# Weight conversion spread over the units, set-up coefficients on GpSimd, in a fused attention and two-MoE kernel

## The chip, the cores and the metric

The kernel runs on one core of one Trainium2 chip. The metric is the device time of one execution in microseconds (us); lower is better. Times of the kernel before are the median and the extremes of three runs, and one further execution that was profiled.

## The reference, cut to what is computed

```
state = alpha[:, :, t, :, None] * state + einsum('bhd,bhe->bhde', k[:, :, t], v[:, :, t])
y[:, :, t] = einsum('bhd,bhde->bhe', q[:, :, t], state)
...
h = x @ w_in
P = a[0] + a[1] * h + a[2] * h2 + a[3] * h3
Q = 1.0 + abs(b[0]) * abs(h) + abs(b[1]) * h2
x2 = (P / (Q + 1e-06)) @ w_out
...
e = exp(h - h_max)
solu = h * e / (sum(e) + 1e-09)
out = layernorm(solu) * g_ln @ w_out
```

A linear attention with a decay per channel (batch 4, 8 heads, 768 steps, width 48) feeds a first layer pair of 384 to 2048 to 384 with a rational function between them, and that feeds a second pair of 384 to 1024 to 384. The last `h`, `w_out` and `out` are the second pair's own. All 3072 tokens go through everything. The matrices come as 64-bit floats.

## The kernel before, in words

**Chunks, halves, units.** The 768 steps are cut into six chunks of 128. A chunk is 512 tokens, 128 of each batch entry. The attention works on half chunks of two batch entries: half 0 and half 1 make chunk 0, half 2 and half 3 chunk 1, and so on to half 11; half 4 is the fifth. The first layer pair works on units. A unit is one chunk of 512 tokens against 128 of the 2048 middle columns, so a chunk has 16 units, and there are 96.

**A unit.** `m_up` (lines 642 to 684) does nine matmuls into a PSUM tile `hp` (line 648), nine because weights and tokens are kept as a high and a low part and three products are added over three row blocks. Then comes a chain: ScalarE writes `ah`, `p` and `w` (lines 653 to 656), VectorE and ScalarE alternate (lines 666 to 679), ScalarE writes the high part `gh` (line 681), GpSimd the low part `gl` (line 682). `MIX(u)` picks one of two forms of the chain: for a mixed unit (lines 666 to 672) VectorE has three passes and GpSimd two more, for another (lines 674 to 679) VectorE has four and GpSimd none. `fin[u]` is the last VectorE pass of the chain (line 672 or 679); it is the last to read `hp`. There are three `hp` buffers, so the matmuls of unit u wait for `fin[u-3]`. `m_down` (lines 686 to 703) adds the unit's share to the output, nine matmuls (line 693), and is written four units behind.

**Conversion of the first pair's weights.** A tile of 64-bit words becomes a 32-bit float by three integer passes on VectorE (lines 540, 543, 544; the first two write `fp`, the third `ft`). ScalarE copies the high part (line 555), and GpSimd subtracts it for the low part (line 560). The weights lie in four groups, one for four units of each chunk, with seven tiles in each: three of `w_in` (512 columns) and four of `w_out` (384 columns). Groups 0 and 1 are converted ahead of unit 0 (`w1_group`), groups 2 and 3 during the units of the first chunk (`w1_slots`, line 585): the loop takes two tiles a unit, group 2 in units 0 to 3 and group 3 in units 4 to 7. For group 2 `fp` is a PSUM tile of the pool `at`, for group 3 it is the SBUF tile `ft` itself. The same passes also convert the second pair's weights from unit 15 on, one tile at a time through `st` (`w2_split`).

**Halves.** Halves 0 and 1 are turned on TensorE with scans on VectorE (`a_turn`, line 343). From half 2 on `a_dve` (line 291) prepares a half on VectorE by block transposes and scans, GpSimd makes the last product (line 327), and the result goes to DRAM (`qk_d`, line 329) and back (`qks`, line 268). `a_pe` (line 396) then does the scores `sc` (line 413), the outputs `y` and the state `u`. `half_steps(i)` interleaves the matmuls of half i with the preparation of half i+1; `HOLD` gives the unit from which that preparation may begin: `{2: (4, 2), 3: (13, 2)}` means that half 3 is prepared from unit 4 on, and half 4 from unit 13.

**Order.** The order of each engine's instructions is settled when the program is built, by a scheduler that works on its own estimate of times. `tc.issue_after(x)` keeps what is written inside it behind the instruction x. `later(n)` uses that with `fin[u-n]`. With `G1 = 99` it holds nothing back in the conversion. Loads go out on one queue (SyncE, SPq in the rows) in the order that the scheduler set.

**Set-up.** `consts` (line 111) loads the coefficients `a` and `b` and makes small vectors of them, 24 instructions of one to four columns on VectorE and ScalarE. `PRE` says how many tiles of group 0 are taken at four places between the loads of halves 0 and 1.

```
if fast and u < NF1:
    if f % 4 == 0:
        _run(prep)
        if f:
            stage["bank"] = ""
        prep = w1_slots(f // 4 + 2) if f < 8 else iter(())
    with later(G1):
        take(prep, 1)
m_up(u)
if fast and u < NF1:
    with later(G1):
        take(prep, 1)
```

Of the kernel before, what the change touches and what calls it, by code (L numbers as in the profile page):

```python
# [30 lines left out]
def kernel(  # L31
# [79 lines left out]
    def consts():  # L111


        nc.sync.dma_start(out=ab, in_=bass.AP(moe_a.tensor, moe_a.offset, [[0, 128], [1, 4]]))
# [7 lines left out]
        nc.vector.tensor_scalar(sign, sign, 1.0, None, ALU.subtract)
        nc.vector.tensor_tensor(lin[:, 1:2], ab[:, 2:3], sign, ALU.mult)
        nc.vector.tensor_tensor(base[:, 1:2], ab[:, 1:2], sign, ALU.mult)
        nc.vector.tensor_tensor(a0s, ab[:, 0:1], sign, ALU.mult)
        nc.vector.memset(base[:, 0:1], QC)
        nc.vector.tensor_scalar(bad[:, 4 * NCH:4 * NCH + 2], cf, C_MIN, None, ALU.is_lt)
        nc.vector.tensor_scalar(cf, cf, C_MIN, None, ALU.max)
# [2 lines left out]
        nc.vector.tensor_tensor(t, beta, beta, ALU.mult)
        nc.vector.tensor_tensor(t, t, cf, ALU.mult)
        nc.vector.tensor_scalar(bad[:, 4 * NCH + 2:], t, BETA * BETA, None, ALU.is_gt)
        nc.vector.tensor_scalar(beta, beta, B_MAX, -B_MAX, ALU.min, ALU.max)
        nc.vector.tensor_tensor(t, beta, beta, ALU.mult)
        nc.vector.tensor_tensor(base, base, rc, ALU.mult)
        nc.vector.tensor_tensor(rest, base, t, ALU.subtract)
# [975 lines left out]
```

## Time and profile before

| what | value |
|---|---|
| median of three runs | 781.0 us (779.27 to 783.73) |
| profiled execution, its own time | 778.71 us |
| its span, first to last instruction | 776.7 us |
| TensorE busy | 731.5 us, 94% of the span |
| VectorE busy | 628.9 us, 81% |
| ScalarE busy | 540.3 us, 70% |
| GpSimd busy | 362.5 us, 47% |
| mean granted TensorE clock | 0.97 |

The profile names engines PE (TensorE), DVE (VectorE), ACT (ScalarE), POOL (GpSimd) and SP (SyncE). A timeline row has the start in us, the time of one or of a merged run of instructions in us, engine, line, operation, output<-inputs, shapes, the count, and in brackets the idle time in front of it and what ended that. The shares above are means over very different stretches: about 80 us in which the attention's first halves and half of the first pair's weights are prepared, the 96 units to about 560 us, and the second pair behind them.

### The profile page before, as it was taken

To read this page: it belongs to the slowest core of one execution; us is meant where nothing else is said; L and a number is where in the kernel's file an instruction comes from. 1 tells how busy PE (TensorE), PEld (TensorE's weight loads), DVE (VectorE), ACT (ScalarE), POOL (GpSimd) and SP (SyncE) were. 2 spreads that over 40 slices of the span, in tenths; PEclk is the share of its full clock that TensorE was granted. 3 is DMA by queue.
4 is the path that set the end of the run, shared out by engine and by line. 5 is a ranking of instruction groups with operands and counts; after the bars stand their busy time and mean duration, and the time that the engine had idled before them with its cause. 6 is when DMAs were issued, how large, how long until landed. Compare 5 with 4: busy or idle time off the path is not lost.

```text
span 776.7 us, 13952 instructions
## 1 busy us (share of the span) xinstructions
PE 731.5 (94%) x4988; PEld 608.4 (78%) x4988; DVE 628.9 (81%) x1097; ACT 540.3 (70%) x998; POOL 362.5 (47%) x314
## 2 busy tenths in 40 slices
PE   4865989999999999999999999999999999999996
PEld 4754777878887787778877788888888989988996
DVE  5997999979998989989898876478887698877630
ACT  3446867867977888788878887788965555555541
POOL 4464878666654355434544433342243343452322
PEclk9957999999999999999999999999999999999999
DMA  7999324275737382717544340730025353541653
GB/s 177 289 295 279 61 81 111 89 224 169 186 121 166 114 207 88 184 47 219 124 144 102 124 82 1 281 127 1 1 82 120 101 131 91 129 111 49 140 118 78
DMA packets 87279, 101.75 MB, mean 131 GB/s; under 512 B 34464, under 2 KB 63136, under 8 KB 87200
## 3 DMA queue, kind: packets, MB, share of 16 engines
q1 hardware_dynamic: 87104, 100.67, 48.0%
q8 instruction: 41, 0.67, 0.4%
q14 instruction: 38, 0.31, 0.1%
q10 hardware_dynamic: 96, 0.10, 0.0%
HBM read 60.59 MB, written 27.56 MB: 113 GB/s over the span
## 4 chain that ended last, share of the span: by engine, by line
DVE 18%; PE 18%; ACT 6%; DMA 3%; SPq 3%; issue 2%; POOL 1%; ACTq 0%; DVEq 0%; POOLq 0%
PE x2p L693 6%; PE hp L648 6%; DVE room L807 3%; SPq L817 3%; DVE room L790 2%; ACT jk L792 2%; PE op L831 2%; DVE sm L786 2%; DVE room L805 2%; PE h L767 2%; DMA L<-room 1%; DVE sm L802 1%; DVE sm L803 1%; DVE p L674 1%; DVE sm L804 1%
## 5 line engine op out<-in xcount | busy, mean ns | idle before, releaser
L682 POOL TENSOR_TENSOR gl<-p,gh 128x512 fp32r<-128x512 f32 x96 | 128.4, 1338 | 198.7 <-ACT gh L681 110.6
L648 PE MATMUL hp<-xt,g 128*128 128x512 f32 x432 | 115.3, 410 | 8.4 <-DVE p L672 7.8
L648 PE MATMUL hp<-xt,w 128*128 128x512 f32 x432 | 110.0, 397 | 4.4 <-DVE p L679 4.4
L648 PEld LDWEIGHTS hp<-xt,g 128*128 128x128 f32 x432 | 82.9, 196 | 29.3 <-DVE p L672 8.0
L831 PE MATMUL op<-w2oh,ln 128*128 128x384 f32 x384 | 101.9, 339 | 0.6 <-DVE ln L823 0.6
L693 PE MATMUL x2p<-gh,g 128*128 128x512 f32 x288 | 100.2, 399 | 2.3 <-ACT x2e L701 2.3
L823 POOL TENSOR_TENSOR ln<-L,ln 128x1024 fp32r<-128x1024 f32 x22 | 54.5, 2482 | 100.8 <-ACT ln L822 96.4
L648 PEld LDWEIGHTS hp<-xt,w 128*128 128x128 f32 x432 | 81.1, 190 | 23.6 <-DVE p L679 5.7
L677 DVE SCALAR_TENSOR_TENSOR w<-w,co,hp 128x512 f32<-128x512 f32 x84 | 62.0, 738 | 44.8 <-ACT hp L676 44.1
L693 PE MATMUL x2p<-gh,w 128*128 128x512 f32 x288 | 96.5, 392 | 0.0
L767 PE MATMUL h<-w2ih,x 128*128 128x512 f32 x288 | 90.8, 394 | 0.0
L655 ACT ACTIVATE p<-hp,co 128x512 f32<-128x512 f32 x96 | 65.8, 685 | 11.1 <-POOL gl L682 10.8
L676 ACT ACTIVATE hp<-ah 128x512 f32<-128x512 f32 x84 | 50.1, 596 | 32.9 <-DVE p L674 32.0
L831 PEld LDWEIGHTS op<-w2oh,ln 128*128 128x128 f32 x384 | 70.1, 188 | 2.2 <-DVE ln L823 1.0
L674 DVE SCALAR_TENSOR_TENSOR p<-p,co,hp 128x512 f32<-128x512 f32 x84 | 61.8, 736 | 9.7 <-ACT p L655 9.1
L656 ACT ACTIVATE w<-ah,co 128x512 f32<-128x512 f32 x96 | 69.3, 723 | 0.4
L693 PEld LDWEIGHTS x2p<-gh,g 128*128 128x128 f32 x288 | 54.6, 191 | 17.5 <-ACT x2e L701 5.0
L653 ACT ACTIVATE ah<-hp 128x512 f32<-128x512 f32 x96 | 56.6, 589 | 14.5 <-PE hp L648 11.5
L681 ACT ACTIVATE gh<-p 128x512 fp32r<-128x512 f32 x96 | 59.9, 624 | 7.9 <-DVE p L679 5.1
L831 PE MATMUL op<-w2ol,ln 128*128 128x384 f32 x192 | 65.0, 339 | 0.0
L693 PEld LDWEIGHTS x2p<-gh,w 128*128 128x128 f32 x288 | 54.1, 188 | 11.7
L767 PEld LDWEIGHTS h<-w2ih,x 128*128 128x128 f32 x288 | 53.9, 188 | 11.7
(183 smaller groups left out, 1569.7 us busy)
## 6 DMA issues: line engine op xcount, KB each, us to landing
L<-room SPq DMA_DIRECT2D x96, 128.0 KB, 2.3
qk_d<-qk SPq DMA_DIRECT2D x10, 771.0 KB, 4.1
st<-in_moe_w_out_dram SPq DMA_DIRECT2D x18, 384.0 KB, 5.0
st<-in_moe_w_in_dram SPq DMA_DIRECT2D x12, 512.0 KB, 4.9
qks<-qk_d SPq DMA_DIRECT2D x20, 257.0 KB, 5.0
ra<-in_alpha_dram SPq DMA_DIRECT2D x48, 96.0 KB, 2.3
rk<-in_k_dram SPq DMA_DIRECT2D x48, 96.0 KB, 2.7
rq<-in_q_dram SPq DMA_DIRECT2D x48, 96.0 KB, 2.4
```

The lines of the kernel that those rows point to most:

```text
L648: last["PE", u] = nc.tensor.matmul(hp, lhsT=wi[n](w, kt, o), rhs=xts[c][:, kt, xx, :], start=(kt == 0 and w == 0 and xx == 0), stop=(kt == ...
L653: nc.scalar.activation(ah, hp, AF.Abs)
L655: nc.scalar.activation(p, hp, AF.Square, bias=co[:, 7:8])
L656: nc.scalar.activation(w, ah, AF.Square, bias=co[:, 6:7])
L674: nc.vector.scalar_tensor_tensor(p, p, a1, hp, ALU.add, ALU.mult)
L677: nc.vector.scalar_tensor_tensor(w, w, rest, hp, ALU.add, ALU.mult)
L681: last["ACT", u] = nc.scalar.activation(gh, p, AF.Copy)
L682: last["POOL", u] = nc.gpsimd.tensor_tensor(gl, p, gh[:].bitcast(F32), ALU.subtract)
L693: nc.tensor.matmul(x2ps[c][d], lhsT=wo[n](w, o, d), rhs=gg, start=(f == 0 and w == 0 and gg is gh), stop=(f == NF1 - 1 and w == 1),)
L767: nc.tensor.matmul(hp[:, 512 * n:512 * n + 512], lhsT=x2s[c][:, kt, x, CH * b:CH * b + CH], rhs=w2[w][:, kt, 512 * n:512 * n + 512], start ...
L823: (nc.vector if s in FASTS else nc.gpsimd).tensor_tensor(lo, L, hi.bitcast(F32), ALU.subtract)
L831: nc.tensor.matmul(op, lhsT=x[:, 128 * f:128 * f + 128], rhs=w2[w][:, f, :], start=(f == 0 and x is hi and w == "oh"), stop=(f == NF2 - 1 ...
```

## The change

- Groups 2 and 3 are taken as one sequence, one tile a unit from unit 1 to unit 15 without unit 11 (`PACE`), after the unit's `m_up`, and held behind `fin[u-2]` (from unit 12 on behind `fin[u-1]`). Their loads are written in units 0 and 3 (`w1_fetch`).
- Units 0 and 2 are no longer mixed.
- The coefficients are computed on GpSimd, one reciprocal excepted, and this is written behind the matmuls of half 0. ScalarE's absolute values become products with a sign.
- The second tile of group 0 is no longer loaded ahead of half 1.
- The preparation of half 4 may begin at unit 14.

```
-    HOLD = {2: (4, 2), 3: (13, 2)}
+    HOLD = {2:(4,2),3:(14,2)}
...
-    PRE = (1, 1, 0, 0)
+    PRE = (1, 0, 0, 0)
...
-    G1 = 99
+    G1 = 2
+    PACE = {u: 1 for u in range(1, 16) if u != 11}
     G2 = 3
-    MIX = lambda u: u < 24 and u % 2 == 0
+    MIX = lambda u: 3 < u < 24 and u % 2 == 0
...
-        nc.scalar.activation(babs, bb, AF.Abs)
+
+    def coefficients():
+
+        sb = const.tile([128, 2], F32, name="sb")
+        nc.gpsimd.tensor_scalar(sb, bb, 0.0, 2.0, ALU.is_ge, ALU.mult)
+        nc.gpsimd.tensor_scalar(sb, sb, 1.0, None, ALU.subtract)
+        nc.gpsimd.tensor_tensor(babs, bb, sb, ALU.mult)
...
-        nc.scalar.activation(cf[:, 0:1], bb[:, 1:2], AF.Abs)
-        nc.scalar.activation(cf[:, 1:2], ab[:, 3:4], AF.Abs)
-        nc.scalar.activation(lin[:, 0:1], bb[:, 0:1], AF.Abs)
-        nc.vector.tensor_scalar(sign, ab[:, 3:4], 0.0, 2.0, ALU.is_ge, ALU.mult)
...
+        nc.gpsimd.tensor_copy(cf[:, 0:1], babs[:, 1:2])
+        nc.gpsimd.tensor_copy(lin[:, 0:1], babs[:, 0:1])
+        nc.gpsimd.tensor_scalar(sign, ab[:, 3:4], 0.0, 2.0, ALU.is_ge, ALU.mult)
...
         nc.vector.reciprocal(rc, cf)
-        nc.vector.scalar_tensor_tensor(beta, lin, 0.5, rc, ALU.mult, ALU.mult)
...
+        nc.gpsimd.tensor_scalar(beta, lin, 0.5, None, ALU.mult)
+        nc.gpsimd.tensor_tensor(beta, beta, rc, ALU.mult)
...
-        def w1_slots(n):
+        words2 = {}
+
+        def w1_fetch(n):
...
+            words2[n] = (order, t, raw)
+
+        def w1_slots(n):
+            if n not in words2:
+                w1_fetch(n)
+            order, t, raw = words2[n]
+            stage["bank"] = "at" if n == 2 and fast else ""
...
-            _run(a_turn(0), a_pe(0), a_turn(1), a_pe(1), pre)
+            _run(a_turn(0), a_pe(0))
+            coefficients()
+            _run(a_turn(1), a_pe(1), pre)
...
                 if fast and u < NF1:
-                    if f % 4 == 0:
-                        _run(prep)
-                        if f:
-                            stage["bank"] = ""
-                        prep = w1_slots(f // 4 + 2) if f < 8 else iter(())
-                    with later(G1):
-                        take(prep, 1)
+                    if f == 0:
+                        w1_fetch(2)
+                        prep = chain(w1_slots(2), w1_slots(3))
+                    if f == 3:
+                        w1_fetch(3)
+                if fast and u == NF1:
+                    _run(prep)
                 m_up(u)
                 if fast and u < NF1:
-                    with later(G1):
-                        take(prep, 1)
+                    with later(G1 if u < NF1 - 4 else 1):
+                        take(prep, PACE.get(u, 0))
```

Lines of the changed program are 8 higher than those of the kernel before up to the weight code (540 becomes 548, 413 becomes 421) and 17 higher behind it (648 becomes 665, 693 becomes 710, 672 and 679 become 689 and 696). Three places show how the built order moves.

**VectorE at the first two units.** From the first rational pass of unit 0 to `fin[0]`. Before:

```order
L674 SCALAR_TENSOR_TENSOR p<-p,co,hp 128x512
L496 TENSOR_TENSOR Sbd<-u,end 48x8x48 x2
L540 TENSOR_SCALAR fp<-words 128x512 x2
L543 SCALAR_TENSOR_TENSOR fp<-words,fp 128x512
L671 SCALAR_TENSOR_TENSOR hp<-hp,co,ah 128x512
L543 SCALAR_TENSOR_TENSOR fp<-words,fp 128x512
L677 SCALAR_TENSOR_TENSOR w<-w,co,hp 128x512
L544 SCALAR_TENSOR_TENSOR ft<-words,fp 128x512
L672 SCALAR_TENSOR_TENSOR p<-w,hp 128x512
```

The last row is `fin[0]`. The same stretch of the changed program:

```order
L691 SCALAR_TENSOR_TENSOR p<-p,co,hp 128x512 x2
L504 TENSOR_TENSOR Sbd<-u,end 48x8x48 x2
L548 TENSOR_SCALAR fp<-words 128x512
L551 SCALAR_TENSOR_TENSOR fp<-words,fp 128x512
L694 SCALAR_TENSOR_TENSOR w<-w,co,hp 128x512
L552 SCALAR_TENSOR_TENSOR ft<-words,fp 128x512
L694 SCALAR_TENSOR_TENSOR w<-w,co,hp 128x512
L695 SCALAR_TENSOR_TENSOR hp<-w,hp 128x512
L691 SCALAR_TENSOR_TENSOR p<-p,co,hp 128x512
L695 SCALAR_TENSOR_TENSOR hp<-w,hp 128x512
L696 SCALAR_TENSOR_TENSOR p<-p,co,hp 128x512
```

One tile's three passes stand there in place of two tiles' five, and four passes of unit 1 and one of unit 2 stand ahead of `fin[0]`.

**TensorE at unit 12**, the first to use group 3 (tiles `w_1004`, `w_1038`, `w_1139` before, `w_1312`, `w_1362`, `w_1405` now). Before, the unit's nine matmuls stand in one piece behind the last `m_down` matmul of unit 7:

```order
L693 MATMUL x2p_1125<-gh,g_649 128x512
L648 MATMUL hp<-xt,w_1004 128x512 x3
L648 MATMUL hp<-xt,w_1038 128x512 x3
L648 MATMUL hp<-xt,w_1139 128x512 x3
L693 MATMUL x2p_1123<-gh,w_872 128x512
```

Now the matmuls of units 12, 13 and 14 stand among each other and among `m_down`, with all of the third tile's at the end:

```order
L665 MATMUL hp<-xt,w_1312 128x512
L665 MATMUL hp<-xt,w_1362 128x512 x2
L421 MATMUL sc<-qks 128x128 x4
L710 MATMUL x2p_1085<-gl,w_1128 128x512
L710 MATMUL x2p_1085<-gh,w_1128 128x512
L710 MATMUL x2p_1086<-gl,w_1128 128x512
L710 MATMUL x2p_1086<-gh,w_1128 128x512
L710 MATMUL x2p_1087<-gl,w_1128 128x512
L665 MATMUL hp<-xt,w_1362 128x512 x2
L710 MATMUL x2p_1087<-gh,w_1128 128x512
L665 MATMUL hp<-xt,w_1312 128x512 x3
L665 MATMUL hp<-xt,w_1405 128x512 x4
```

Ahead of the third tile's first matmul stand `m_down` of units 8 and 9.

**TensorE at the fifth half's scores** (`sc` of half 4). Before, they follow `m_down` of unit 15, and `m_up` of unit 19 comes behind them:

```order
L693 MATMUL x2p_1125<-gh,w_1199 128x512
L693 MATMUL x2p_1125<-gl,w_1199 128x512
L693 MATMUL x2p_1125<-gh,w_1233 128x512
L413 MATMUL sc<-qks 128x128 x8
L648 MATMUL hp<-xt,g_136 128x512 x9
L693 MATMUL x2p_2125<-gh,g_136 128x512
```

Now they stand behind `m_up` of unit 21 and `m_down` of unit 17:

```order
L665 MATMUL hp<-xt,g_653 128x512 x9
L710 MATMUL x2p_2129<-gh,g_136 128x512
L710 MATMUL x2p_2129<-gl,g_136 128x512
L710 MATMUL x2p_2129<-gh,g_136 128x512 x2
L710 MATMUL x2p_2129<-gl,g_136 128x512
L710 MATMUL x2p_2129<-gh,g_136 128x512
L421 MATMUL sc<-qks 128x128 x8
```

Five groups of nine matmuls have come in front of them: `m_up` of units 19 to 21, `m_down` of 16 and 17.

## Rows read from the trace of the kernel before

**Rows 1.** Three stretches: length, busy PE, PEld, DVE, ACT, POOL; clock, DMA share, GB/s.

```profile
75.20:155.50 80.30, 76.27 (x557) 60.98 (x558) 79.84 (x126) 63.20 (x119) 63.68 (x59) 0.94 0.34 89
20.00:62.50 42.50, 34.30 (x348) 28.50 (x345) 42.04 (x91) 18.12 (x39) 21.63 (x21) 0.72 1.01 287
97.00:137.00 40.00, 36.02 (x287) 28.72 (x287) 39.84 (x55) 27.77 (x52) 32.18 (x27) 0.96 0.33 93
```

**Rows 2.** TensorE's waits over the span: total us, times, longest us.

```profile
PE hp L648 <- DVE p L672: 7.8, 1, 7.8
PE hp L648 <- DVE p L679: 4.6, 4, 4.0
```

**Rows 3.** TensorE's timeline around units 9 and 10 and the fifth half's scores.

```profile
109.12 2.23 PE L648 MATMUL hp<-xt,w 128*128 128x512 f32 x9
111.19 0.39 PE L693 MATMUL x2p<-gh,g 128*128 128x512 f32 x1
...
118.42 3.85 PE L648 MATMUL hp<-xt,w 128*128 128x512 f32 x9 [3.98 <-DVE p L679]
...
172.02 1.13 PE L413 MATMUL sc<-qks 48*128 48x128 f32 x8 [1.30 <-DMA qks<-qk_d]
173.08 3.89 PE L648 MATMUL hp<-xt,g 128*128 128x512 f32 x9
```

**Rows 4.** VectorE's timeline at six places (waits in brackets).

```profile
27.50 0.68 DVE L540 TENSOR_SCALAR fp<-st 128x512 int32<-128x512 int32 x1
...
65.54 0.76 DVE L666 SCALAR_TENSOR_TENSOR hp<-p,co,hp 128x512 f32<-128x512 f32 x1 [2.48 <-ACT p L655]
...
69.95 1.29 DVE L540 TENSOR_SCALAR fp<-words 128x512 int32<-128x512 int32 x2 [1.38 <-DMA words<-in_moe_w_in_dram]
...
74.51 0.68 DVE L672 SCALAR_TENSOR_TENSOR p<-w,hp 128x512 f32<-128x512 f32 x1
75.11 0.75 DVE L666 SCALAR_TENSOR_TENSOR hp<-p,co,hp 128x512 f32<-128x512 f32 x1
75.77 0.68 DVE L544 SCALAR_TENSOR_TENSOR ft<-words,fp 128x512 int32<-128x512 int32 x1
...
130.64 1.12 DVE L493 TENSOR_TENSOR Sbd<-Sbd,u 48x384 f32<-48x384 f32 x2
...
154.84 0.62 DVE L282 STREAM_TRANSPOSE qk<-rq 128x256 f32<-128x256 f32 x1
```

**Rows 5.** The load queue's timeline: issues in the start, and halves 3 and 4 through DRAM.

```profile
4.55 1.85 SPq L258 DMA_DIRECT2D rq<-in_q_dram  x4
...
11.77 0.43 SPq L533 DMA_DIRECT2D st<-in_moe_w_in_dram  x1
...
19.77 1.06 SPq L340 DMA_DIRECT2D vn<-in_v_dram  x2
...
118.97 1.72 SPq L268 DMA_DIRECT2D qks<-qk_d  x4
...
157.92 0.39 SPq L329 DMA_DIRECT2D qk_d<-qk  x1
```

**Rows 6.** The tile `st`, 0 to 70 us: its loads from issue to landing.

```profile
DMA to landing us min/median/max: 4.3/5.8/8.2
```

**Rows 7.** GpSimd's timeline: one small copy, the last products of halves 3 and 4.

```profile
17.47 0.19 POOL L427 COPY end<-qks 128x8 f32<-128x8 f32 x1
...
113.08 1.75 POOL L327 TENSOR_TENSOR qk<-qk,P 128x768 f32<-128x768 f32 x1 [0.91 <-DVE qk L282]
...
156.14 1.75 POOL L327 TENSOR_TENSOR qk<-qk,P 128x768 f32<-128x768 f32 x1
```

**Rows 8.** The tile `words`, 0 to 140 us, group 3's passes: ns min/median/max, first and last start.

```profile
L540 DVE TENSOR_SCALAR ft<-words x6: 347/652/871, 97.7 to 127.7; 128x512 int32<-128x512 int32 x3, 128x384 int32<-128x384 int32 x3
L543 DVE SCALAR_TENSOR_TENSOR ft<-words,ft x6: 546/928/1529, 101.5 to 129.5; 128x512 int32<-128x512 int32 x3, 128x384 int32<-128x384 int32 x3
L544 DVE SCALAR_TENSOR_TENSOR ft<-words,ft x6: 559/1650/1879, 105.8 to 131.8; 128x512 int32<-128x512 int32 x3, 128x384 int32<-128x384 int32 x3
```

More of the change, by code (lines that the diff above doesn't have):

```diff
@@ L122, in consts @@
[L122 to L128, printed above, removed]
-        nc.vector.reciprocal(rc, cf)
@@ L130, in consts @@
-        nc.vector.scalar_tensor_tensor(beta, lin, 0.5, rc, ALU.mult, ALU.mult)
[L131 to L137, printed above, removed]
@@ L138, in consts @@
-        nc.vector.tensor_tensor(a0s, a0s, rc[:, 1:2], ALU.mult)
-        nc.vector.tensor_tensor(back, cf[:, 1:2], rc[:, 0:1], ALU.mult)
-        nc.vector.tensor_tensor(back, back, sign, ALU.mult)
+    def coefficients():
[3 more added lines that the diff above has]
+        nc.gpsimd.tensor_tensor(babs, bb, sb, ALU.mult)
+        cf, lin, rc, beta, rest, t, base = (co[:, 2 * x:2 * x + 2] for x in range(7))
+        nc.gpsimd.tensor_copy(cf[:, 0:1], babs[:, 1:2])
+        nc.gpsimd.tensor_copy(lin[:, 0:1], babs[:, 0:1])
+        nc.gpsimd.tensor_scalar(sign, ab[:, 3:4], 0.0, 2.0, ALU.is_ge, ALU.mult)
+        nc.gpsimd.tensor_scalar(sign, sign, 1.0, None, ALU.subtract)
+        nc.gpsimd.tensor_tensor(cf[:, 1:2], ab[:, 3:4], sign, ALU.mult)
+        nc.gpsimd.tensor_tensor(lin[:, 1:2], ab[:, 2:3], sign, ALU.mult)
+        nc.gpsimd.tensor_tensor(base[:, 1:2], ab[:, 1:2], sign, ALU.mult)
+        nc.gpsimd.tensor_tensor(a0s, ab[:, 0:1], sign, ALU.mult)
+        nc.gpsimd.memset(base[:, 0:1], QC)
+        nc.gpsimd.tensor_scalar(bad[:, 4 * NCH:4 * NCH + 2], cf, C_MIN, None, ALU.is_lt)
+        nc.gpsimd.tensor_scalar(cf, cf, C_MIN, None, ALU.max)
+        nc.vector.reciprocal(rc, cf)
+        nc.gpsimd.tensor_scalar(beta, lin, 0.5, None, ALU.mult)
+        nc.gpsimd.tensor_tensor(beta, beta, rc, ALU.mult)
+        nc.gpsimd.tensor_tensor(t, beta, beta, ALU.mult)
+        nc.gpsimd.tensor_tensor(t, t, cf, ALU.mult)
+        nc.gpsimd.tensor_scalar(bad[:, 4 * NCH + 2:], t, BETA * BETA, None, ALU.is_gt)
+        nc.gpsimd.tensor_scalar(beta, beta, B_MAX, -B_MAX, ALU.min, ALU.max)
+        nc.gpsimd.tensor_tensor(t, beta, beta, ALU.mult)
+        nc.gpsimd.tensor_tensor(base, base, rc, ALU.mult)
+        nc.gpsimd.tensor_tensor(rest, base, t, ALU.subtract)
+        nc.gpsimd.tensor_tensor(a0s, a0s, rc[:, 1:2], ALU.mult)
+        nc.gpsimd.tensor_tensor(back, cf[:, 1:2], rc[:, 0:1], ALU.mult)
+        nc.gpsimd.tensor_tensor(back, back, sign, ALU.mult)
@@ L899, in pin @@
             if n <= now[0] < NU and fast:
-                for e, u in (("PE", now[0]), ("ACT", now[0] - n), ("POOL", now[0] - n)):
+                for e, u in (("PE", now[0] if ("PE", now[0]) in last else now[0] - 1), ("ACT", now[0] - n), ("POOL", now[0] - n)):
                     stack.enter_context(tc.issue_after(last[e, u].ins))
```

## The prediction

> **What bounds the kernel now.** I read the busy time by stretches first. From 20 to 62.5 us VectorE is busy 42.04 of 42.50 us, while TensorE has 34.30 at a mean clock of 0.72; from 75.2 to 155.5 us VectorE has 79.84 of 80.30 and TensorE 76.27 [rows 1]. So up to about 155 us VectorE is the bound, and TensorE runs dense only where VectorE lets it. Next the waits of TensorE: one of 7.8 us on the last pass of unit 0's chain, and 4.6 in four on the other form's last pass, of which one is 3.98 [rows 2, 3]. Then the timeline there. The 3.98 stand in front of unit 10 at 118.42, and the matmuls behind them take 3.85 us where nine at full speed take 2.23, so another 1.6 goes to the half clock. The fifth half's scores wait 1.30 us for their data at 172.02, and the group behind takes 3.89 [rows 3]. Behind that the page's slices show TensorE near full to the end. The change works on what lies before 172 us; what it is worth is when TensorE is done there.
>
> I sum against the profiled execution, 778.71 us. The median, 781.0, stands 2.3 above it. An effect under 0.5%, 3.9 us, can't be told from none.
>
> **The start.** VectorE comes to group 0's third tile at 27.50 us and is dense from there [rows 4]. The change takes the second tile's load (issued at 11.77) from in front of half 1's twelve input loads and two v loads, and issues it behind them. Four such loads take 1.85 us to issue and the two v loads 1.06 [rows 5], so from 11.77 the tile is issued at 11.77 + 3 x 1.85 + 1.06 = 18.4, and with the median of 5.8 us to land it is there at 24.2 [rows 6]. VectorE has half 1's first scans to do meanwhile, as the coefficients and the second tile no longer stand among them. So the dense stretch begins at 24.2 in place of 27.5, 3.3 earlier, but with the second tile's three passes still to do, 0.60 to 0.66 each by the starts of neighbouring rows [rows 4], 1.9 together. **Gain 1.4.** With landing in 4.3 it is 2.9; with 8.2 a loss of 1.0 [rows 6].
>
> The coefficients become 26 GpSimd instructions. The nearest row is a small copy of 0.19 us [rows 7], so some 5 us on an engine that is busy 21.63 of 42.5 us there [rows 1]. Nine of them stand ahead of half 0's last product, which gives back a buffer that half 1's first scan needs; at 0.19 that is 1.7 us, and VectorE waits for the tile until 24.2 in any case. I cost it at nothing. If the product were late by more than the wait for the tile, it would eat into the 1.4.
>
> **The first chains.** The 7.8 us wait ends with the last pass of unit 0. Its place is set by the first tile of group 2, whose words land at 69.95, and by the passes in front [rows 4]. The order shown keeps that tile's first pass ahead, and puts three conversion passes and five of units 0, 1 and 2 before `fin[0]`: four spacings of 0.66 and four of 0.60 make 5.0, so it starts at 75.0 where it started at 74.5 [rows 4]. This wait stays, 0.4 longer. The later chains come earlier, but TensorE is busy then. Units 0 and 2 without mixing give VectorE one pass each, and the first of them is in this count.
>
> **The wait in front of unit 10.** Between `fin[0]` and `fin[7]` about 30 us of VectorE passes stand in the new order, so `fin[7]` falls at 75.6 + 30 = 106, while TensorE comes there no earlier than 114. Both the 3.98 and the 1.6 of half clock go: 5.6 us at that place.
>
> **Where they come back.** VectorE's work is not less, it is moved back. From `fin[0]` to the last transposes of half 4 it needs 80.3 us before (75.2 to 155.5, dense). Counted in both orders, the new one has more in that stretch: 9 passes of chains (0.66), 2 of group 2 (0.60), 5 of the second pair's first tiles (0.65) and 2 of `Sbd` (1.12 for two) [rows 4], together 11.5 us. So the last transposes end at 75.6 + 80.3 + 11.5 = 167.4, less the start's 1.4. To that I add VectorE's own waiting. Its least is none. Its most I put at 7: units 8, 9 and 12, where little conversion stands between the passes of a chain, could each wait for ScalarE as unit 0 does, 2.48 us [rows 4]. I take 1.5, nearer to the 0.5 of the whole stretch before [rows 1], because elsewhere the conversions fill the chains' gaps.
>
> From the transposes to the scores lie GpSimd's product of 1.75 us, the write to DRAM and the read back. For half 4 it was 155.5 to 172.0, 16.5 us; for half 3 the product began at 113.08, the reads were issued at 118.97 over 1.72, and with the 4 us that a write from 114.9 to 118.9 took they were there near 124.7, 11.6 us [rows 5, 7]. I take 14. The scores are then ready at 167.4 - 1.4 + 1.5 + 14 = 181.5.
>
> In the new order TensorE has five more groups of nine matmuls in front of them, 2.07 each by the starts of two rows [rows 3], 10.3. The same point of its work was 172.0 + 10.3 = 182.3. **The difference is -0.8.** TensorE is ahead by the 5.6 and the 1.4 at unit 11, and gives that back at unit 12, where the third tile of group 3 is ready about when its first matmul comes (a near tie, 0 to 3 us), at unit 16, whose `fin[13]` stands only just ahead of half 4's transposes, and at the scores. Behind the scores the work and its order are alike, and the clock falls once as before. That half 4 may begin a unit later is in the count of passes; the moved loads are issued in nearly the old order, so they cost nothing while VectorE is behind them.
>
> Sum: 778.7 - 0.8, and 781.0 - 0.8 = 780.2 for the median.
>
> **A rule against the rows.** Group 3's passes read and write SBUF alone, and last 0.65, 0.93 and 1.65 us in the median where their least is 0.35, 0.55 and 0.56 [rows 8]; GpSimd is busy 32.18 of 40 us around them [rows 1]. The Trainium skill, SBUF — State Buffer, section "SBUF: two separate sides", says that VectorE and GpSimd share one port pair, which one instruction holds to its end while the other waits. By that, how much a tile costs is decided by the GpSimd pass it meets, and spreading the tiles saves nothing as long as GpSimd is as full as before, which leaves the sum at 780.2; without such a hold the first rival would be the likelier case. The rows fit the rule, but none shows the port itself.
>
> **Rivals.**
>
> *The tiles fall into gaps (faster, 0.30).* If group 3's passes ran near their least, six tiles would save up to 6 x (0.30 + 0.38 + 1.09) = 10.6 us of VectorE time [rows 8]. Half 4 would be ready at 171, and TensorE would be the bound: its work to the scores, 172.0 - 1.3 - 5.6 + 10.3 - 1.4 = 174.0, against 182.3. That is 8.3 less, 772 for the median. For it: the tiles come one a unit and behind a finished chain. Against it: GpSimd's 80%, and that its work per unit stays, but for units 0 and 2.
>
> *The fifth half comes late (slower, 0.22).* VectorE waits its 7 us around units 8 to 12, half 4's data needs the 16.5 of before, and the start gains nothing: 167.4 + 7 + 16.5 = 190.9 against 182.3, 8.6 more, 789. It decides from the point where the last transposes end later than 168. For it: two chains (units 9 and 12) need GpSimd passes and ScalarE copies that stand behind conversion work, and SPq's order has the reads behind transfers of the second pair. Against it: the whole stretch had only 0.5 us of waiting before [rows 1].
>
> *The start doesn't move (no change, 0.08).* The tile lands as late as 26.6, and all else holds: 780.2 + 1.4 + 1.0 = 782.6.
>
> **How the numbers follow.** My forecast, VectorE's work moved back and the time as it was, has 0.40, and its own range is 776 to 785 (chain 11.6 or 16.5 and waiting 0 to 4). Of it 0.04 fall below 777.1 and 0.02 above 784.9. So faster by over 0.5%: 0.30 + 0.04 = 0.34, less 0.01 for the weak end of the first rival; slower: 0.22 + 0.02 = 0.24; the rest, 0.43, no change. The range of 772 to 788 takes in the first rival in full and most of the second.
>
> **What would show it.** Right, if the 3.98 in front of unit 10 is gone, VectorE is as full from 75 to 165 us as before, and TensorE has new waits at unit 12, unit 16 or the scores that sum to 5 to 8 us, with the scores at 180 to 183. The start is right if VectorE's dense stretch begins near 24 and `fin[0]` ends near 74. Wrong, if TensorE has no wait over 1 us between units 4 and 22, if group 3's third passes have a median under 1 us, or if the time changes behind the fifth half.

## The result and the profile after

The changed kernel takes **789.3 us** in the median (786.91 to 793.35, 13 runs) against 781.9 for the kernel before (777.65 to 786.93, 13 runs): a ratio of 1.0102 [1.0082, 1.0123]. It is slower by 1%, above the range of 772 to 788. The profiled executions have spans of 787.2 and 776.7 us, 10.5 apart; the medians are 7.4 apart, and the profiled execution of the kernel before took 3.2 us less than its median. Two of e12's four times below were disturbed (over 1.4 ms), so that kernel was measured again as e15, and one of e11's ten (2.4 ms) is left out of its ratio.

The windows of the kernel after, over the stretch of [rows 1] and over four stretches (columns as there):

```profile
77.90:177.50 99.60, 90.66 (x648) 72.53 (x649) 90.87 (x145) 72.49 (x135) 67.94 (x63) 0.92 0.29 76
60.00:100.00 40.00, 30.37 (x162) 23.95 (x161) 33.67 (x58) 29.54 (x54) 19.65 (x19) 0.84 0.64 187
100.00:140.00 40.00, 39.46 (x310) 31.96 (x309) 36.24 (x53) 26.45 (x50) 31.03 (x29) 1.00 0.35 93
140.00:160.00 20.00, 13.52 (x185) 11.14 (x184) 15.48 (x24) 15.92 (x31) 11.92 (x11) 0.88 0.18 41
160.00:200.00 40.00, 34.70 (x141) 26.22 (x142) 37.20 (x67) 29.40 (x56) 25.15 (x23) 0.89 0.66 192
```

The same four stretches of the kernel before:

```profile
60.00:100.00 40.00, 32.16 (x167) 25.80 (x166) 35.44 (x66) 31.31 (x60) 28.03 (x28) 0.86 0.61 168
100.00:140.00 40.00, 36.02 (x287) 28.74 (x286) 39.73 (x55) 27.80 (x52) 31.75 (x28) 0.96 0.35 96
140.00:160.00 20.00, 20.00 (x211) 15.94 (x210) 19.01 (x31) 15.58 (x31) 14.20 (x13) 1.00 0.33 102
160.00:200.00 40.00, 38.70 (x310) 31.41 (x307) 35.28 (x56) 30.78 (x56) 26.32 (x25) 0.96 0.69 194
```

What TensorE loses in a stretch, idle or at the half clock, is the length less busy time times granted clock. From 60 to 100 us it is 40 - 32.16 x 0.86 = 12.3 before and 40 - 30.37 x 0.84 = 14.5 after; from 100 to 140, 5.4 and 0.5; from 140 to 160, 0.0 and 8.1; from 160 to 200, 2.8 and 9.1. Together 20.5 and 32.2, so 11.7 more, against the 10.5 of the spans. So the whole loss of this pair of executions lies ahead of 200 us, and it is what is left of a gain of 4.9 and losses of 2.2, 8.1 and 6.3.

TensorE's waits and timeline after (answers to [rows 2, 3]):

```profile
PE hp L665 <- DVE p L696: 10.6, 4, 9.6
PE hp L665 <- DVE p L689: 9.5, 3, 6.5
```

```profile
107.30 2.23 PE L665 MATMUL hp<-xt,w 128*128 128x512 f32 x9
...
111.77 2.22 PE L665 MATMUL hp<-xt,w 128*128 128x512 f32 x9
...
115.87 2.20 PE L665 MATMUL hp<-xt,w 128*128 128x512 f32 x9
...
159.72 6.96 PE L665 MATMUL hp<-xt,g 128*128 128x512 f32 x18 [6.48 <-DVE p L689]
...
177.01 2.37 PE L665 MATMUL hp<-xt,g 128*128 128x512 f32 x9 [1.06 <-DVE p L689]
...
188.17 3.43 PE L665 MATMUL hp<-xt,g 128*128 128x512 f32 x9 [1.91 <-DVE p L689]
...
193.41 1.71 PE L421 MATMUL sc<-qks 48*128 48x128 f32 x16
```

The 3.98 us in front of unit 10 are gone, and units 8 to 10 run at 2.2 us each. In their place stand 6.48 us at 159.72, and behind them 18 matmuls that take 6.96 us where two groups of nine take 4.4, 1.06 at 177.01 and 1.91 at 188.17. Half 4's scores come at 193.41. They do not wait for their data there; they stand behind the unit that waited at 188.17.

VectorE's timeline after (answers to [rows 4]):

```profile
26.68 0.70 DVE L548 TENSOR_SCALAR fp<-st 128x512 int32<-128x512 int32 x1 [3.31 <-DMA st<-in_moe_w_in_dram]
...
66.47 0.75 DVE L691 SCALAR_TENSOR_TENSOR p<-p,co,hp 128x512 f32<-128x512 f32 x1 [2.95 <-ACT p L672]
...
71.93 0.69 DVE L548 TENSOR_SCALAR fp<-words 128x512 int32<-128x512 int32 x1 [2.44 <-DMA words<-in_moe_w_in_dram]
...
77.16 0.74 DVE L696 SCALAR_TENSOR_TENSOR p<-p,co,hp 128x512 f32<-128x512 f32 x1
...
142.33 0.76 DVE L683 SCALAR_TENSOR_TENSOR hp<-p,co,hp 128x512 f32<-128x512 f32 x1 [2.82 <-ACT p L672]
144.35 0.76 DVE L688 SCALAR_TENSOR_TENSOR hp<-hp,co,ah 128x512 f32<-128x512 f32 x1 [1.27 <-ACT ah L685]
145.86 0.69 DVE L689 SCALAR_TENSOR_TENSOR p<-w,hp 128x512 f32<-128x512 f32 x1 [0.75 <-POOL w L687]
...
147.81 0.68 DVE L691 SCALAR_TENSOR_TENSOR p<-p,co,hp 128x512 f32<-128x512 f32 x1
...
150.29 0.74 DVE L683 SCALAR_TENSOR_TENSOR hp<-p,co,hp 128x512 f32<-128x512 f32 x1
...
151.36 2.52 DVE L308 TENSOR_TENSOR_SCAN P<-alT,d 128x774 f32<-128x774 f32 x1
153.81 0.67 DVE L548 TENSOR_SCALAR fp<-st 128x512 int32<-128x512 int32 x1
...
155.12 0.74 DVE L694 SCALAR_TENSOR_TENSOR w<-w,co,hp 128x512 f32<-128x512 f32 x1
...
156.93 0.76 DVE L688 SCALAR_TENSOR_TENSOR hp<-hp,co,ah 128x512 f32<-128x512 f32 x1
157.60 0.69 DVE L695 SCALAR_TENSOR_TENSOR hp<-w,hp 128x512 f32<-128x512 f32 x1
...
158.98 0.68 DVE L689 SCALAR_TENSOR_TENSOR p<-w,hp 128x512 f32<-128x512 f32 x1
...
160.06 0.68 DVE L696 SCALAR_TENSOR_TENSOR p<-p,co,hp 128x512 f32<-128x512 f32 x1
...
176.88 0.63 DVE L290 STREAM_TRANSPOSE qk<-rq 128x256 f32<-128x256 f32 x1
```

The tile lands at 26.68, and `fin[0]` is done at 77.9. Unit 12's chain (142.33 to 145.86) makes VectorE wait three times, 4.84 us together. Unit 13's chain has its first pass at 147.81 and its second at 155.12. Between them stand the scan of half 4 and passes on the second pair's first tile, among others, without any idle time: VectorE takes its queue in order. `fin[13]` starts at 160.06. Unit 14's chain is drawn out in the same way, from its first pass at 150.29 to its second at 156.93, and `fin[14]` (L689) starts at 158.98. It is this pass that ends the 6.48 us: it is done at 159.66, ahead of `fin[13]`. So the matmuls of unit u do not always wait for `fin[u-3]`: in this order unit 16 takes the `hp` buffer that unit 14 gives back, and unit 17, the second nine of the 18 matmuls, the one of unit 13. Before, the four passes of unit 13's chain stood close together:

```profile
146.01 0.68 DVE L674 SCALAR_TENSOR_TENSOR p<-p,co,hp 128x512 f32<-128x512 f32 x1
...
148.30 0.71 DVE L677 SCALAR_TENSOR_TENSOR w<-w,co,hp 128x512 f32<-128x512 f32 x1
...
149.81 0.68 DVE L678 SCALAR_TENSOR_TENSOR hp<-w,hp 128x512 f32<-128x512 f32 x1
...
151.06 0.73 DVE L679 SCALAR_TENSOR_TENSOR p<-p,co,hp 128x512 f32<-128x512 f32 x1
```

### The profile page after: what moved, and what is told of

The parts are those of the page before. It is cut to its first block, busy times and chain, and to the rows that moved or that the text cites. A ratio compares the mean times of both kernels' runs of the same rounds, so it can differ in the third digit from the quotient of the medians.

```text
span 787.2 us, 13935 instructions
## 1 busy us (share of the span) xinstructions
PE 733.3 (93%) x4988; PEld 610.1 (78%) x4988; DVE 625.7 (79%) x1080; ACT 540.7 (69%) x994; POOL 359.8 (46%) x336
## 4 chain that ended last, share of the span: by engine, by line
PE 42%; DVE 30%; ACT 10%; issue 6%; DMA 6%; SPq 4%; POOL 2%; DVEq 0%; ACTq 0%; POOLq 0%
PE x2p L710 11%; PE hp L665 11%; PE h L784 9%; PE op L848 8%; SPq L266 3%; DVE w L694 2%; DVE p L691 2%; DVE hp L695 2%; DMA words<-in_moe_w_in_dram 2%; DMA rq<-in_q_dram 2%; DVE fp L548 2%; DVE qk L290 2%; ACT hp L693 2%; DVE p L696 2%; DVE alT L324 1%
## 5 line engine op out<-in xcount | busy, mean ns | idle before, releaser
L665 PE MATMUL hp<-xt,g 128*128 128x512 f32 x432 | 118.7, 418 | 19.9 <-DVE p L696 10.2
L665 PEld LDWEIGHTS hp<-xt,g 128*128 128x128 f32 x432 | 84.8, 201 | 42.2 <-DVE p L696 12.5
L672 ACT ACTIVATE p<-hp,co 128x512 f32<-128x512 f32 x96 | 65.9, 687 | 10.4 <-POOL gl L699 10.2
L691 DVE SCALAR_TENSOR_TENSOR p<-p,co,hp 128x512 f32<-128x512 f32 x86 | 63.1, 734 | 11.5 <-ACT p L672 11.1
L696 DVE SCALAR_TENSOR_TENSOR p<-p,co,hp 128x512 f32<-128x512 f32 x86 | 63.5, 738 | 1.1
```

What stands on the lines that cost most here:

```text
L665: last["PE", u] = nc.tensor.matmul(hp, lhsT=wi[n](w, kt, o), rhs=xts[c][:, kt, xx, :], start=(kt == 0 and w == 0 and xx == 0), stop=(kt == ...
L672: nc.scalar.activation(p, hp, AF.Square, bias=co[:, 7:8])
L691: nc.vector.scalar_tensor_tensor(p, p, a1, hp, ALU.add, ALU.mult)
L696: fin[u] = nc.vector.scalar_tensor_tensor(p, p, a0, hp, ALU.add, ALU.mult)
```

## The experiments

Three theories stood at the start. Theory 1: the pacing leaves VectorE waiting behind unit 0 and piles its work up in front of units 16 to 21. Theory 2: the start, whose loads land later, makes the loss. Theory 3: unit 14 for half 4 makes it.

Times are medians; the ratio is to the kernel before, run beside each kernel, with its 95% interval. The losses are TensorE's, worked out as above from each kernel's own windows. "Half 4" is where GpSimd's last product of half 4 starts (in `before`, 156.14 in [rows 7]).

| kernel | us | ratio | 60-100 | 100-140 | 140-160 | 160-200 | half 4 |
|---|---|---|---|---|---|---|---|
| before | 781.9 | 1 | 12.3 | 5.4 | 0.0 | 2.8 | 156.1 |
| after | 789.3 | 1.0102 [1.0082, 1.0123] | 14.5 | 0.5 | 8.1 | 9.1 | 177.6 |
| e1 | 790.2 | 1.0093 [1.0063, 1.0123] | 18.3 | 7.9 | 0.4 | 7.3 | 168.1 |
| e2 | 788.5 | 1.0063 [1.0038, 1.0088] | 10.2 | 0.6 | 9.7 | 9.8 | 163.5 |
| e3 | 792.1 | 1.0129 [1.0088, 1.0171] | 13.7 | 0.9 | 7.0 | 9.5 | 177.7 |
| e4 | 786.8 | 1.0066 [1.0041, 1.0090] | 17.1 | 0.5 | 8.0 | 5.9 | 165.1 |
| e5 | 787.4 | 1.0055 [1.0032, 1.0078] | 18.0 | 4.7 | 0.7 | 8.3 | 162.5 |
| e6 | 781.3 | 0.9983 [0.9958, 1.0008] | 13.5 | 1.6 | 6.7 | 3.7 | 146.1 |
| e7 | 786.1 | 1.0038 [1.0011, 1.0065] | 16.7 | 3.2 | 0.4 | 6.0 | 163.8 |
| e8 | 785.1 | 1.0027 [1.0003, 1.0051] | 13.6 | 0.5 | 7.5 | 7.0 | 172.8 |
| e9 | 784.7 | 1.0042 [1.0017, 1.0067] | 11.0 | 1.2 | 7.9 | 5.3 | 146.3 |
| e10 | 780.8 | 0.9971 [0.9947, 0.9996] | 16.2 | 4.2 | 1.9 | 0.8 | 156.5 |
| e11 | 784.6 | 1.0033 [1.0008, 1.0057] | 13.2 | 1.5 | 7.5 | 5.3 | 145.3 |
| e13 | 784.1 | 1.0013 [0.9990, 1.0036] | 11.4 | 7.6 | 1.8 | 2.2 | 155.8 |
| e14 | 778.6 | 0.9961 [0.9939, 0.9984] | 13.1 | 3.7 | 2.0 | 1.1 | 154.1 |
| e15 | 789.2 | 1.0072 [1.0047, 1.0097] | 11.4 | 7.6 | 0.7 | 10.0 | 163.4 |
| e16 | 791.4 | 1.0102 [1.0067, 1.0137] | 13.8 | 3.4 | 9.5 | 6.5 | 156.9 |
| e17 | 789.9 | 1.0089 [1.0068, 1.0110] | 16.1 | 0.5 | 4.6 | 12.2 | 166.1 |

after, e4, e6, e8 and e11 are written alike up to unit 11 and differ by up to 4 in the first column (13.2 to 17.1), so that column tells little apart. Each row's losses and half 4 are of one execution, and it was not always near the median: 3.2 us less in before, 5.0 more in e5, 3.7 more in e1, 2.7 less in e3. e12 and e15 are one kernel: 14.1 and 11.4, 5.5 and 7.6, 0.4 and 0.7, 9.7 and 10.0.

**Parts of the change, one taken out.** e1 undoes the pacing:

```
-                    with later(G1 if u < NF1 - 4 else 1):
-                        take(prep, PACE.get(u, 0))
+                    with later(G1):
+                        take(prep, 1)
```

(and the loop ahead of `m_up` as before, with `G1 = 99`).

> The change without its pacing: groups 2 and 3 again two tiles a unit in units 0 to 7 with their loads written there; start, unmixed units 0 and 2 and unit 14 as in the change. Theory 1 (the spread conversion leaves VectorE waiting at units 8 to 12 and puts the work in front of units 16 to 21): most of the 7.4 us come back, 780 to 784, half 4's last transposes near 158, a wait of some 4 us in front of unit 10 again, none over 2 us at units 16 to 21. Theory 2 (the later loads of the start cost 2.7 us at the last pass of unit 0's chain): that loss stays, with the last pass of unit 0 at 77 to 78, so 784 to 785. Theory 3 (unit 14 for half 4): nothing comes back, 789.

The 8.1 at 140 to 160 are gone (0.4) and the losses from 100 to 140 are back (7.9), as theory 1 has it. But nothing comes back in the time, 790.2: half 4 is still late, and unit 0's wait is 12.9 us. The pacing is a cause, and not the only one.

e3 undoes the start (`PRE`, and `consts` on VectorE and ScalarE):

> The change with the old start: coefficients on VectorE and ScalarE ahead of half 0, two tiles of group 0 taken early. Theory 1: VectorE's work behind unit 0 is the same, so at most the start's 2.7 us come back: 786 to 789, TensorE's wait at units 16 and 17 still over 5 us. Theory 2: exactly the 2.7 at the last pass of unit 0 come back and are carried to the end, 786.6; if they are eaten by the waits at units 16 to 21, 789.

792.1, no better than the change, so theory 2 falls: that the tile lands late makes none of the loss that these times could show. TensorE's wait on `fin[0]` is 8.7 in place of 9.6, and half 4 is as late as in the change.

e4 has half 4 from unit 13 again:

```
-    HOLD = {2:(4,2),3:(14,2)}
+    HOLD = {2:(4,2),3:(13,2)}
```

> The change with half 4 prepared from unit 13 again. Theory 1: half 4's passes only move ahead of the passes of unit 13, whose lateness then makes the wait at unit 16, so 787 to 790. Theory 3 (the later hold makes half 4 late): half 4's last transposes come 3 us or more earlier than 176.9 and the time falls to 783 to 786.

Half 4's product starts 12.5 earlier and TensorE loses 3.2 less from 160 to 200. The time falls by 2.5, between the two theories, with intervals that touch.

**Parts alone.** e2 is the kernel before with the pacing (fetch, one tile a unit, hold), e5 with units 0 and 2 unmixed (`MIX = lambda u: 3 < u < 24 and u % 2 == 0`), e12 and e15 with unit 14 for half 4 (`3: (14, 2)`). They also take over one line of the change that the cuts above leave out, on what a part of a half's preparation is kept behind when its unit's own matmuls are not yet written. Of these kernels only those with unit 14 come to that case.

> The kernel before with the pacing alone (fetch, one tile a unit, held behind the unit two back). Theory 1: the loss is here, 786 to 789, with waits of TensorE at units 16 to 21 of over 6 us in sum and half 4's last transposes later than 170. Theory 2: the last pass of unit 0 ends near 75.2 as before, so the time is at most 2.7 us better than the change, and if the start were all of the loss, 782. Theory 3: no loss, 782.

> The kernel before with units 0 and 2 unmixed, and nothing else changed. If the loss needs the pacing or the later half 4, the time stays within 0.5% of 782 (two passes more on VectorE and two pairs less on GpSimd near unit 0, 1.3 us at most). If the unmixed units are by themselves a cause, TensorE's wait on the last pass of unit 0's chain grows from 7.8 us to 9 or more and the time is 784 to 786.

> The kernel before with half 4 prepared from unit 14 in place of 13, and nothing else. Theory 1 (the later half costs only what VectorE's fill behind unit 12 makes of it): before, VectorE has fewer passes there, so half 4's data comes some 3 us later and the scores wait 3 to 5 us instead of 1.3: 784 to 786. If the later half costs nothing without the pacing: 781 to 783.

> Unit 14 for half 4 in the kernel before, alone, once more, because two of the four times of the first run of it were disturbed. If its two other times (787.7 and 790.7) are the kernel's own, the median is 787 to 791, half 4's last product starts near 165 and TensorE loses some 10 us between 140 and 200 us where it lost 3. If they too were disturbed: 781 to 783.

The pacing alone costs 0.6%. It has all of the gain at 100 to 140 and loses 9.7 and 9.8 behind it. The unmixed units alone cost 0.55%, where I had one pass of 0.66 us for each. In the profiled execution, which took 5.0 us more than e5's median, unit 0's wait is 13.45 us and half 4's product starts 6.4 later; which of the two makes the loss is not shown. e5's TensorE row:

```profile
80.10 3.90 PE L648 MATMUL hp<-xt,g 128*128 128x512 f32 x9 [13.45 <-DVE p L679]
```

Unit 14 alone costs 0.72%, 5.6 us (6.9 by the medians): one number, which moves half 4's product by 7.3 us. e12's profile reads the same (164.8, and 9.7 lost from 160 to 200). e15's scores of half 4, which wait for their data now:

```profile
178.74 1.17 PE L413 MATMUL sc<-qks 48*128 48x128 f32 x8 [3.29 <-DMA qks<-qk_d]
180.81 2.04 PE L413 MATMUL sc<-qks 48*128 48x128 f32 x8 [0.90 <-DMA qks<-qk_d]
```

Where a good part of the 7.3 comes from can be read on VectorE. Besides the unit, `HOLD` names a distance, 2: each part of the preparation is also kept behind the last pass of the chain two units back. Half 4's first instruction stands behind `fin[11]` in the kernel before, and behind `fin[12]` in e15:

```profile
137.61 0.75 DVE L679 SCALAR_TENSOR_TENSOR p<-p,co,hp 128x512 f32<-128x512 f32 x1
138.31 0.07 DVE L294 MEMSET alT<- 128x12 f32 x1
```

```profile
142.88 0.69 DVE L672 SCALAR_TENSOR_TENSOR p<-w,hp 128x512 f32<-128x512 f32 x1 [0.75 <-POOL w L670]
143.52 0.07 DVE L294 MEMSET alT<- 128x12 f32 x1
```

So the half begins 5.2 later. Of this 1.5 are e15's being late already (its `fin[11]` starts at 139.13), and 3.7 are the one chain more that it is kept behind.

So three parts lose 0.63, 0.55 and 0.72% alone, 1.9% together, and the whole loses 1.0%. The times do not add up. Half 4's lateness does: 7.4, 6.4 and 7.3 alone, 21.1 together, and 21.5 in the change. So the loss does not grow with the lateness; why, no run shows.

**Half 4 earlier, other work away.** e6 is the change with `3:(11,2)`, e7 with `PACE = {u: 2 for u in range(1, 8)}`, e8 with `U2, IDLE = NF1 + 7, (0, NF1 // 2 - 1)`, e10 with e7's `PACE` and `3:(12,2)`, e11 with e6's and e8's edits.

> The change with half 4 prepared from unit 11 in place of 14. Theory 1, as the traces so far read: VectorE stands idle 8.7 us behind unit 0 because the pacing left it only chain passes there, and the same passes then stand in front of units 13 and 14. With half 4's passes written from unit 11 they fill the waits of unit 12: half 4's last transposes by 168 at the latest (176.9 in the change, 167 with unit 13), the wait at units 16 and 17 under 4 us, the scores by 180, the time 781 to 785. The rival (the waits of unit 12 are set by ScalarE's order of copies alone): the wait stays at 6 to 7 us and the time at 786 to 789.

> The change with two tiles a unit in units 1 to 7 in place of one a unit to unit 15; fetch, hold behind the unit two back, unit 14 for half 4, start and unmixed units stay. If the lateness of the tiles is the loss, group 3 is done by about 125 us as before (131.8), unit 12 finds ScalarE free of copies, the wait at units 16 and 17 falls under 3 us, and a wait in front of units 9 to 11 comes back with 2 to 4 us: 783 to 786. If holding the tiles behind a finished chain is the loss and not their number a unit, the time stays at 788 to 790.

> The change with the second pair's first tiles taken from unit 23 in place of unit 15, so that no pass on them stands among units 13 to 21. Eight to eleven VectorE passes of 0.55 to 0.70 us leave the stretch from 153 to 178, 5 to 7 us. If the stretch is bound by the number of VectorE's passes, half 4's last transposes end near 171 and the time falls by 4 to 6, to 783 to 785. If it is bound by the chains' order (unit 13's passes behind half 4's scan), the wait at units 16 and 17 stays over 5 us and less than 2 us come back: 787 to 789.

> The change with both: two tiles a unit in units 1 to 7, and half 4 prepared from unit 12 in place of 14. Two tiles a unit with unit 14 took 786.1, with TensorE's losses between 160 and 180 us. If half 4's place is what is left of the loss there, the time is 779 to 783 and the scores of half 4 find their data (no wait over 1 us); if the passes of group 3 are in the way wherever they stand, 785 to 788.

> The change with half 4 prepared from unit 11 and the second pair's first tiles from unit 23. Each alone brought 789.3 to 781.3 and to 785.1. If both take work out of the same full stretch of VectorE between 145 and 180 us, they add up in part: 777 to 781, and TensorE's wait at unit 16 falls under 4 us. If the wait at unit 16 is the latency of unit 12's and 13's chains and not the amount of work, nothing is added: 781 to 784.

e6 takes back the whole loss (781.3) by one number. At 140 to 160 it still loses 6.7, though not by the same wait: TensorE waits 2.35 us in front of 150.66 and 3.00 in front of 160.93. What goes is the loss behind it, 9.1 to 3.7. In e7 it is the other way round: the 8.1 go to 0.4, and 6.0 are left behind. e10 does both, and both go. e8 and e11 leave the first where it was; e8 takes 785.1 all the same, with 7.0 behind it, and e11 adds nothing to e6. e10's windows:

```profile
140.00:160.00 20.00, 18.12 (x176) 13.90 (x175) 17.14 (x27) 14.87 (x30) 13.67 (x12) 1.00 0.31 95
160.00:200.00 40.00, 39.19 (x338) 31.94 (x338) 36.59 (x59) 32.29 (x60) 26.92 (x25) 1.00 0.75 200
```

**On the kernel before.** e9 is before with the pacing and unit 11, e13 with unit 12 alone (`3: (12, 2)`), e14 with e7's `PACE`, the fetch and hold of the change and unit 12.

> The kernel before with two things of the change or near it: the pacing, and half 4 prepared from unit 11 instead of 13. Start and mixed units are those of before. With unit 13 the pacing alone took 788.5, with unit 11 the whole change took 781.3. If half 4's place decides, this comes to 776 to 780: the first chain's wait stays at 7 us or less (6.9 in the pacing alone, 9.6 in the whole change), the wait in front of unit 10 is gone, the one at unit 16 under 6 us. If it is the unmixed units 0 and 2 that made unit 11 work, the time stays at 784 to 788.

> The kernel before with half 4 prepared from unit 12 in place of 13, and nothing else. Over the kernels so far the time goes with the start of GpSimd's last product of half 4: 781 where it starts by 156.5 (the kernel before: 156.1), 785 to 792 where it starts later than 162. If an earlier half 4 is worth as much as a later one costs, it starts near 150 and the time is 776 to 780. If 156 is early enough and the scores are then bound by TensorE's own work, the time is 780 to 783.

> The kernel before with the fetch and the hold of the change, two tiles a unit in units 1 to 7, and half 4 prepared from unit 12; coefficients, tile loads of the start and mixed units as before. The same with the change's start and unmixed units took 780.8, with 41.3 us of TensorE lost by 100 us of which unit 0's wait of 11.0 is a part. If the mixed units 0 and 2 only shorten that wait to 7 or 8 us, the time is 777 to 780. If they bring the wait in front of unit 10 back, with 4 to 6 us, it is 781 to 784.

e13 leaves half 4 where it was (155.8) and gains nothing. e9 still has the 7.9 of the pacing. **e14 is faster than both kernels, 778.6**, than the kernel before by 0.4% (e10, with the change's start and unmixed units, by 0.3%, with an interval that ends at 0.9996; the two can't be told apart). Group 3's last pass starts at 133.2 us, half 4's product starts at 154.1, and from 140 to 200 us TensorE loses 3.1.

**Work taken away, order kept.** e16 is e14, e17 the change, with group 3's intermediate in PSUM:

```
-            stage["bank"] = "at" if n == 2 and fast else ""
+            stage["bank"] = "at" if fast else ""
```

> The kernel of e14 with the intermediate of group 3's passes in a PSUM tile, as group 2 has it, instead of SBUF. Group 2's passes there have medians of 0.62 us each and least values of 0.55; group 3's 0.69, 0.78 and 0.96 with up to 1.67. If what lengthens them is that they read and write SBUF alone while GpSimd works, six tiles take 6 x (0.07 + 0.16 + 0.34) = 3.4 us less of VectorE, the losses at 100 to 200 us fall by 1 to 3 and the time is 776 to 779. If the PSUM tiles are wanted by the attention's halves at that time, TensorE gets new waits on them and the time is 780 to 786. The first passes, which take 0.35 at their least from SBUF, can become longer.

> The change with the same: group 3's intermediate in PSUM. Group 3's passes there have medians of 0.81, 1.13 and 1.07 us; at 0.62 each six tiles take 6 x 1.15 = 6.9 us less of VectorE between 121 and 166 us. If VectorE's amount of work in that stretch makes TensorE's wait at unit 16, the loss of 8.1 us at 140 to 160 falls under 4 and the time is 783 to 786. If it is the order of the passes and the waiting of unit 12's chain, it stays at 6 to 9 and the time at 786 to 790.

e16's time misses both of its cases, and e17 has the time of its second with a loss, 4.6, that neither had. Group 3's passes in the kernel after, and all twelve tiles' in e17 (the tile `words`, ns min/median/max, first and last start):

```profile
L548 DVE TENSOR_SCALAR ft<-words x6: 344/814/1505, 121.2 to 160.7; 128x512 int32<-128x512 int32 x3, 128x384 int32<-128x384 int32 x3
L551 DVE SCALAR_TENSOR_TENSOR ft<-words,ft x6: 557/1132/1683, 124.2 to 163.3; 128x512 int32<-128x512 int32 x3, 128x384 int32<-128x384 int32 x3
L552 DVE SCALAR_TENSOR_TENSOR ft<-words,ft x6: 540/1074/1322, 125.8 to 165.6; 128x512 int32<-128x512 int32 x3, 128x384 int32<-128x384 int32 x3
```

```profile
L548 DVE TENSOR_SCALAR fp<-words x12: 550/652/694, 69.9 to 156.0; 128x512 int32<-128x512 int32 x6, 128x384 int32<-128x384 int32 x6
L551 DVE SCALAR_TENSOR_TENSOR fp<-words,fp x12: 547/622/695, 70.6 to 159.0; 128x512 int32<-128x512 int32 x6, 128x384 int32<-128x384 int32 x6
L552 DVE SCALAR_TENSOR_TENSOR ft<-words,fp x12: 526/618/687, 72.0 to 163.9; 128x512 int32<-128x512 int32 x6, 128x384 int32<-128x384 int32 x6
```

The passes became as short as expected: no median over 0.66 and no pass over 0.70 us. The time did not move. VectorE now waits for the PSUM tile itself, 5.28 us until ScalarE has read a score tile of the same pool:

```profile
135.16 0.56 DVE L548 TENSOR_SCALAR fp<-words 128x384 int32<-128x384 int32 x1 [5.28 <-ACT A L428]
```

The 8.1 became 4.6, and the 9.1 behind them 12.2. e16's TensorE waits 5.18 us in front of scores, and the end of a VectorE pass of group 3 stands just ahead:

```profile
145.52 0.56 DVE L545 SCALAR_TENSOR_TENSOR ft<-words,fp 128x384 int32<-128x384 int32 x1
```

```profile
146.17 2.04 PE L414 MATMUL sc<-qks 48*128 48x128 f32 x8 [5.18 <-issue]
```

The profile names no cause for this wait. In the built program these scores wait for that very pass, which reads `fp`, a tile of the pool `at` that the scores use too, and it ends at 146.08. So this is the wait of e16's second case, TensorE on the PSUM tiles, and its 791.4 lie beyond the 780 to 786 given for it.

## Why the prediction was wrong

*The start: gain 1.4.* The tile landed at 26.68, the late end of my bounds (26.6), and in e4, e6, e8, e11 and e17, which are written alike to there, at 25.7 to 26.1: the gain was not there. `fin[0]` ended 2.7 later than before, and I had 0.4. Of that 2.0 are the landing of group 2's first tile, 71.93 against 69.95, and this scatters: those five kernels have 68.9 to 71.2. e3 shows no loss from the start. What the coefficients cost by themselves was not tested.

*The wait in front of unit 10: 5.6 back.* Right: 4.9 less lost from 100 to 140 us, in the change and in every kernel with one tile a unit (0.5 to 1.6).

*VectorE's work, 11.5 more.* Right: 80.3 + 11.5 = 91.8, and 90.87 us of busy time were measured from 77.90 to 177.50.

*From the transposes to the data: 14.* Right: half 4's reads were issued until 185.9 us and took 5.7 to 7.0 to land, so the data was there some 14 to 15 us behind the transposes.

**VectorE's own waiting: 1.5.** This is the first step that failed. It was 99.60 - 90.87 = 8.7, above even my bound of 7; unit 12's chain alone has 4.84. The last transposes ended at 177.5, where I had 167.5: 7.2 of these 10.0 are the waiting, 3.7 the later `fin[0]`, and the work gives 0.9 back. I took the small value because the stretch before had 0.5. But that stretch was full because conversion passes stood in every gap, and the change thins out those passes and holds them: from unit 12 on a tile may not start before the chain of the unit before it is done. The next tile's first pass started at 146.47, right behind unit 12's chain, so nothing was there to fill its 4.84. No run drops this hold alone.

**"That half 4 may begin a unit later is in the count of passes."** The second one. It was costed at nothing, and e15 measures 5.6 us for it in the kernel before. The count of passes in front of half 4's last transposes is one thing; the chain that each part of half 4 is kept behind is another, and it moves with the unit, 3.7 us for its first part.

**What TensorE gives back.** I had 5.6 + 1.4 returned at units 12 and 16 and at the scores, so that all three share one debt. Unit 12 and the scores had no wait of over 1 us. Unit 16 had one, as I said, of 6.48 us, but on `fin[14]` where I had `fin[13]`. TensorE lost 8.1 around it and 6.3 more than before behind it. These are two debts. Every kernel with one tile a unit and group 3 in SBUF alone (after, e2, e3, e4, e6, e8, e9, e11) loses 6.7 to 9.7 from 140 to 160 us wherever half 4 stands, and those with two a unit 0.0 to 2.0; with PSUM between, e17 (one a unit) loses 4.6 and e16 (two a unit) 9.5, with its 5.18 at the scores. Every kernel whose half 4 starts its product later than 162 loses 6 to 12 from 160 to 200, with the pacing or without. The reverse does not hold: e9 and e11 have half 4 by 147 and lose 5.3. One edit removes one and leaves the other (e6, e7), and both are gone in e10 and e14. Why the first one appears, I can only argue: with no tile free to run, VectorE waits out unit 12's chain, the work that was held back then stands between the passes of units 13 and 14, and the second pass of each comes 7.3 and 6.6 us behind its first. e17 speaks against the mere amount of work, but as it brought a wait of its own, it does not settle it.

*The rivals.* The fifth half came late, as the slower rival had it: transposes at 176.9, behind its point of 168, and 789 was its time. Its sum was right in size, though it put all of it on the scores' data and had nothing at unit 16. *The tiles fall into gaps* is refuted by the rows above: the medians of group 3's three passes add up to 3.02 us, where [rows 8] has 3.23.

*The rule against the rows.* The Trainium skill, SBUF — State Buffer, section "SBUF: two separate sides", has VectorE and GpSimd share one port pair that one instruction holds to its end. The Trainium skill says it of a VectorE instruction with two SBUF inputs or in a mode that uses two ports. The trace agrees more plainly now: with PSUM between them the same passes take 0.62 to 0.65 us in the median and none over 0.70, with SBUF alone up to 1.68 (e17 and the kernel after). In the kernel after the first pass on a tile of 384 columns takes 1.45 us at 135.75, when GpSimd has a pass from 135.26 to 136.98, and 0.35 at 146.47, when GpSimd stands idle from 145.83 to 147.93. The port itself is in no row.

## What to carry to other kernels

When filler work is spread thinner over an in-order engine, count its own waiting anew: a stretch that was full only because of the filler has the latency of each chain in it once the filler is gone. A start time in such a program (here the unit from which a half is prepared) is not a detail that goes with the count of work; try it alone and together with the change, as one step of it was worth 5.6 us here. And when parts of a change each lose alone, look for the one thing they all delay, here half 4, and count the loss anew for the whole: the delays added up and the losses did not.

## What the runs showed that I had not expected

- One integer, the unit from which half 4 may be prepared, was worth 8.0 us in the change (e6, three units earlier, 781.3 against 789.3) and 5.6 us in the kernel before (e15, one unit later), but nothing there one unit earlier (e13).
- Integer passes of 384 and 512 columns took 0.34 to 1.68 us between SBUF tiles and 0.53 to 0.70 with PSUM between (after, e17). The shorter passes bought no time: VectorE waited 5.28 us for a PSUM tile in e17, and TensorE 5.18 us in e16.
